# Attention with streaming heads, then a SwiGLU block: masks and sums shared between VectorE and GpSimd, scaling split in two, another written order

## The chip, the cores and the metric

The kernel runs on one core of one Trainium2 chip. A core has TensorE (PE, matrix products), VectorE (DVE), ScalarE (ACT), GpSimd (POOL) and SyncE (SP, which here only starts transfers). Each engine takes its own instructions strictly in order; semaphores make one wait for another. The metric is the device time of one execution, in microseconds (us).

## What is computed

Four batches, eight heads, 768 positions, 64 values a head. Three heads look at all earlier keys, five ("streaming") at four sink keys and a window of 64. The result is laid out as 3072 rows of 512 and goes through a gated feed-forward block of width 1536.

```python
scores = scale * np.matmul(q, k.transpose(0, 1, 3, 2))
stream_keep = causal & (is_sink | in_win)
mask = np.where(retr[0, :, 0, 0, None, None], full_mask, stream_mask)
scores = np.where(mask[None, :, :, :], scores, -1000000000.0)
a = np.exp(scores - np.max(scores, axis=-1, keepdims=True))
a = a / (np.sum(a, axis=-1, keepdims=True) + 1e-09)
attn = np.matmul(a, v)                       # -> x: 3072 x 512
g = x @ w_gate
out = (g * (1.0 / (1.0 + np.exp(-g))) * (x @ w_val)) @ w_out
```

## The kernel before

**Tiles.** The 3072 rows are 24 tiles of 128. Tiles come in pairs (tiles 2n and 2n+1 of pair n), with one load each of q, k and v (v is called x in the load names). Four tiles make a group for the feed-forward block; there are six groups, 0 to 5.

**Attention.** For each pair q and k are cast to f16 (`cq`, `ck`), turned by PE (`trq`, `trk`, L466) and copied out of PSUM (`evq`, `evk`); v is cast (`cx`, four pieces). For each tile there are two to four units of scores. PE makes a unit (`sc`, L560, matmuls that use 64 rows), ACT takes the exponential (`ex`, L569), and POOL multiplies units 0 and 1 by a 0/1 mask (`mask`, L577; for the first four tiles PE adds the mask itself). PE then makes the values (`val`, L587, odd heads and even heads), with a column of ones that yields the sum. DVE takes the reciprocal of these sums and scales (`nm`: L594 and L595 in one task), PE turns the result (`xtr`, L606), and it is copied out as the group's input (`xe`). `sk` and `sv` copy the sink keys and values beside each key tile.

**Feed-forward.** For each of a group's 12 blocks j PE makes a gate and a value product (`gate`, `vals`, L732; four matmuls of 512 columns, in group 0 for j under 4 in halves of 256). ACT makes a tanh (L738), DVE two fused multiplications (`stt1` L742, `stt2` L748), which leave h in f16. Groups 0 to 4 use a fast product: seven block products (`p1` to `p7`, L812) in place of eight, for which sums of blocks of h (`hs`, L799, each in two parts of 768 columns) and of the output weights (`ws`, L412, 512 columns) are needed. DVE adds the products up (`oe`, L828), and SP or ACT stores them. Group 5 uses the plain product (L766), so that the end is short.

**Weights.** Six loads each of the gate, value and output weights (`load g`, `v`, `o`), cast to f16 by one of three engines (`wc`).

**Order.** Nothing is scheduled at run time or by the compiler. Every task is added with a list of engines that may do it, what it depends on, and the buffers it takes. Three strings then say everything: `ORDER` is the order in which all tasks are issued (two characters a task), `WAYS` picks the engine from the task's list (0 is its first), `SLOTS` the buffer of each ring. Numbers over 3700 in `ORDER` are warm-ups: matmuls on the identity whose result nobody uses. Since every engine is in order, `ORDER` also sets what waits behind what on it.

**Buffers.** PSUM is eight banks (`gv`, `o` take one, `big` takes two). A bank is free for the next gate when its `stt` has run.

Of the kernel before, what the change touches and what calls it, by code (L numbers as in the profile page):

```python
# [13 lines left out]


ORDER = (
    "0706090A0C001W1X02041U1V03xx1f1gy21c1h2021yG28292A1d1e011i1j051p1q1r1w1s22232B2C2DzG2E2F2N2O2L2M"
    "2S2W2c2d081b1Z1a1Y1t1u1v1k1l1m0D2X2f2g2o2h2p2i0B2624252G2H272I2P2Q0G3D2j2k2l2t2m2n0F1n2R1y2J2K1z"
    "1o2U2V0m11103C3I3J3K2e2x2y30311x9G9L0g0y9D9E9F980z9I9J9H9K9M999A0h9B9C3L3M3N139X9Y9Z9S9T9U9c9d9e"
    "32383R3S3O9N9O0n149V9W9P9a9b9k9f9g0E2Y2Z2b2a2q3P2r2s2u0o179p9h9i9j9l0i169m9n9o9q3b33343U3V9r9s9t"  # L20
    "9Q9R2z353637390k1C3i3j0l1FALAMAN3Q9u9v3T0j3W3X3f3gAGAHAI3l3n0H3E3F3Y3Z3m3o3a3GABACA6A72v3A0q1DA9"
    "199w3h0r1G3H3k0K3x3y3wA8AA9x9yAOAPAJAKA10I3uAE0J3v3c3pA20p2w0w1E3dADAFATAV3B1A0s123q3r3z4344450x"
    "1HA3409zA03s3tA44142494A4647484B3eB4BEB7B5B6BdBFBGBeB8BgA5ASAU0v1B1KAx0u181Q4H4O4C4DBfBh0M4bAuAv"
    "Aw0S0t151M1OAyBJBKBL4L4M4WBTBUBV0L4aBM2TBC0Y7E4P4QApAqBWBXB9BABBBDArBN1SBYBZBaAQAXARAW4j4k4lBbBc"
    "Bi1IBjBk1R1T4g4h4i0V4E4F4GBHBI1N1P1J1L0O5IAsAt0P5J0R4R4S4N4m4n4o0Q5N5K5M4s4t0W6X0N4c4d4eAeAYAa4p"
    "4z4q4rAZAzB0B1B2B35p5R5S5T53AcAdAi0eAfAj0UAgAhAkAo4I4T54554U4V4XBOBPBQ0ZBlBm56574u4v5O5P5QBRBS5v"
    "5w5x584w4x4y50BnBo595A5B5C5f5gBv5q4J4K51524f5D5E7I5FAbAlAm5G5H4Y5c5l5dBp0T5u5s6Y5U5VBqBsC50c5h0f"
    "4ZCMCNCOD5D6ClCoD7CmCnCp5yBrC1AnBw5t5z60617F627M7N7OD0D1D264656CBtBxD8D9CbCcCdBuByBzC0666G6H6ZC2"
    "C66J6R5L6WD3D4C3C4C7CBCgChCi5e5i6K5j5m5kCvCwCPCQCx6e6f6gCjCk5W5X5Y5Z7HCCCDCECyCz6M6N67686V6b6c6d"
    "7m6aCeCf6L630X8TCFCG5r696A6B6DC8C95a5n5o5b6E6F6I6O6P6S6QCHCICJCqCrCs8R7D7J7K7L6T6UCA6h6i6jCtCu7n"  # L30
    "CWCXCYCKCLDCDE0a7kEDEEEFCRCSCTEGEHENEOEP6p6qCZCa6n6o6k6u6l6mCUCVDDDFDeDfDg7176777P7Q7REIEJEKELEM"
    "DhDi6r6s6t6v7273EQERESET0b7l7q7r7sDADGDBDHEU7a7b7c7X7Y7Z7g7t7u7v6w6xDyDzE0E1E2DZDaDbDtDuDvDcDd74"
    "756yDwDxDMDN7G7S7T7d7e7f6z707UDoDpDqDIDJDKDL7z80817o82837wDjDkDlDrDsE8E9EA8Z8a8b78797x7y7A7i7jE3"
    "7p8SE67BEBEC7V7WDODPEVEW7h848586E4E5E70d8Q7CF9FLFMFN8U878E8F8G8H8IDQDRFOFP8W8X8B8C8DDSDUDYDTFEDV"
    "DWDX8YDmDn8M8c8k8l8d8eFfFgFhFaFbFcEaFBFCFDFFFdFe8f8p8gFpFqFrF6F7F8FAEfEXEYEgFQ888J8K8L8i8j8NEZEb"
    "FGFHFI8V8hEdEhFn8w8x8y9192FkFlFiFjFmFoFsFtFRFS8m8n8oEwExFVFWFXFJFK8qFTFU8z908t8uEcElEeEiEsEjEkEm"
    "F1F2F3EnEo898r8A8s8O8v9394Ep959697EzF48PGsEyF0GgGqErEvFxEqH0GtGuGxGyFzEtEuGbF5GzH1GdGeGfGhGnGoGp"
    "GrGRGYGZGaGOGPH2H3GcGQGSH4H7H8FYFZH9FwFyGvGwGlFuG0FvGiGjGkGWGmGAGTGUGVGXH5H6HFGJGKGLG1G6G7HAG2G3"
    "G4G5GMGNG8G9GBHBGCHCHDHEHGGFGDGGGHGEGIHHHIHJHMHNHKHLHOHRHSHTHWHUHXHPHQHVHYHZHbHaHcHd"
)  # L40
WAYS = (
    "000011000000000000000000000000000000000000000000000000000000221222212202000222120000000000001212"
    "222200000000000000000000000010222212011011000000000000002200222202010000000000000000001000000000"
    "001000022220011000000000000000002000000000000000000202000000000000000000002000000000000000001111"
    "020000000000000000000020000000000000000111002100001000000001000000000020100200001000000000000000"
    "020000000000000220022110000000000000000000000101000000000000001200020001011000000000000000001200"
    "010221000011000000000001201000000000001001201020000010000000000000020000000000000000000000000000"
    "000000000000000000000000000000000000000000000000000000000000000000000000000000000000000000000000"
    "000000000000000000000000000000000000000000000000000000000000100000000000000000000000000000000000"
    "000000000000000000000000000000000000000000000000000000000000000000000000000000000000000000000000"  # L50
    "000000000000000000000000000000000000001000000000000000000000100000000000000000000000000000000000"
    "000000000000000000000000000100000000000000000000011000000000000000000000000000000000000000000000"
    "00000000000000000000000110000000000001"
)
SLOTS = (
    "010523746398924140017A691538054937A26015867A243A0728A5610106041104122604230063425254461240012220"
    "616021634560623213222642160414454362206033410246145620040626321320124465214360460626441622432440"
    "621165236020212616240613644563623432261644260400045616443601212225622426021013212562406111646123"
    "602404160624445624226160436133025200041115011401001041120010140250100510251151104002111142021000"
    "105010103111210300242114110200231013211051242020002001131000011010421000101111021203013411510201"  # L60
    "101101230243003552112201121013112000112013502441205021100020210100201431500242103300140100104010"
    "0112151133105202030222114230520231200001302031053100312120042120200121014011300412010"
)
# [56 lines left out]
def kernel(  # L120
# [89 lines left out]
    def recast(task, dst, src):  # L210
# [370 lines left out]
    def values(t, odd):  # L581
        if t not in avs:
            avs[t] = buf("big", [128, 2, 512], FP, "av")
        for n in range(4):
            bl = av_blocks.pop((t, 2 * n + odd))
            for m, (ee, vv) in enumerate(bl):
                nc.tensor.matmul(avs[t][:, odd, n * 66:n * 66 + 65], ee, vv,  # L587
                                 start=(m == 0), stop=(m == len(bl) - 1))

    def norm(t):  # L590
        xb = xbs[t] = buf("xb", [128, 4, 2, 64], FH, "xb")
        rc = small.tile([128, 2, 4, 1], FP, name="rc", tag="rc")
# [1 line left out]
        nc.vector.reciprocal(out=rc, in_=av[:, :, :, 64:65])  # L594
        nc.vector.tensor_tensor(  # L595
            out=xb.rearrange("p n o d -> p o n d"), in0=av[:, :, :, 0:64],
            in1=rc.to_broadcast([128, 2, 4, 64]), op=ALU.mult)
# [395 lines left out]
```

## Time and profile before

| what | us |
|---|---|
| median of three runs (255.04 to 255.12) | 255.06 |
| the profiled execution's own time | 255.12 |
| its span, first to last instruction | 253.3 |
| PE busy | 245.6 |
| POOL busy | 187.1 |
| DVE busy | 179.9 |
| ACT busy | 159.0 |

The span is shorter than the time by what lies before the first instruction and after the last. Busy time of PE includes the flight of a matmul through the array, so successive matmuls of 512 columns show as 379 ns each while they start every 216 ns. The page cuts the span into 40 slices of 6.3 us; a digit is the busy share in tenths. In the groups, a line is: source line, engine, operation, out<-in by the program's names, shapes, count, then busy us and the mean ns of one, then the idle time before it and what ended that. In the chain, a line is start, length, engine, tile and line.

### The profile page before, as it was taken

Reading aid. Unit: us, or ns where it says so; the run is one execution under the profiler, and the core shown is the slowest. Engines: PE = TensorE matmul, PEld = TensorE weight load, DVE = VectorE, ACT = ScalarE, POOL = GpSimd, SP = SyncE. Lnnn points to the kernel's source line nnn. Section 1 sums busy time; section 2 is a strip of 40 time slices with the busy share of each in tenths; the row PEclk is TensorE's granted clock in tenths of the full one; section 3 lists DMA queues with packets and bytes.
Section 4 is the critical chain, followed back from the end, with each engine's and each line's share of the span. In section 5 each row is a group of like instructions: output and inputs, shape, how many; then the busy total and the mean of one; then the engine's idle time right before and its main releaser. Section 6 shows DMA issues by size and latency. Waiting matters only on the chain.

```text
span 253.3 us, 5948 instructions
## 1 busy us (share of the span) xinstructions
PE 245.6 (97%) x2367; PEld 153.3 (61%) x2367; DVE 179.9 (71%) x319; ACT 159.0 (63%) x256; POOL 187.1 (74%) x168
## 2 busy tenths in 40 slices
PE   7988999999999999999999999999999999999995
PEld 2666855554566786665654657666465774466743
DVE  1469789759899964888676767785686576875740
ACT  5797879988767689867996675644746222511002
POOL 6689999899999999999638997856699532073400
PEclk9999999999999999999999999999999999999999
DMA  7999999999930294005270000002200004000053
GB/s 193 359 353 338 346 330 354 385 387 355 311 121 0 72 280 150 5 0 168 71 262 0 3 0 3 0 3 82 86 4 0 3 0 155 14 0 3 0 194 137
DMA packets 32331, 34.98 MB, mean 138 GB/s; under 512 B 1456, under 2 KB 22192, under 8 KB 32304
## 3 DMA queue, kind: packets, MB, share of 16 engines
q1 hardware_dynamic: 31200, 32.71, 40.3%
q10 hardware_dynamic: 1104, 1.90, 2.0%
q8 instruction: 18, 0.29, 0.5%
q14 instruction: 9, 0.07, 0.1%
HBM read 28.31 MB, written 6.29 MB: 137 GB/s over the span
## 4 chain that ended last, share of the span: by engine, by line
PE 58%; POOL 26%; SPq 4%; issue 3%; DMA 3%; ACT 2%; DVE 2%; POOLq 0%; DVEq 0%; ACTq 0%
PE banks L732 33%; PE banks L812 11%; POOL e L577 9%; POOL h_sb L799 7%; POOL wt_sb L412 5%; PE banks L766 4%; PE banks L560 4%; PE banks L587 4%; SPq L349 3%; DMA raw<-in_k_dram 3%; POOL hs_sb L799 2%; PE banks L466 1%; POOL vt L208 1%; PE banks L606 1%; DVE sil L742 1%
## 5 line engine op out<-in xcount | busy, mean ns | idle before, releaser
L577 POOL TENSOR_TENSOR e<-e,m 128x1024 f16<-128x1024 f16 (+1 forms) x38 | 67.3, 1783 | 19.2 <-ACT e L569 19.2
L738 ACT ACTIVATE sig<-banks 128x512 f32<-128x512 f32 (+1 forms) x76 | 43.2, 577 | 50.3 <-PE banks L732 39.0
L732 PE MATMUL banks<-xt,wv_sb 128*128 128x512 f16 (+1 forms) x304 | 72.0, 368 | 0.3 <-POOL wv_sb L208 0.2
L569 ACT ACTIVATE e<-banks 128x1024 f16<-128x1024 f32 (+2 forms) x68 | 59.5, 910 | 20.0 <-PE banks L560 10.9
L732 PE MATMUL banks<-xt,wg_sb 128*128 128x512 f16 (+1 forms) x304 | 71.5, 368 | 0.1
L742 DVE SCALAR_TENSOR_TENSOR sil<-sig,banks 128x512 f32<-128x512 f32 (+1 forms) x76 | 49.4, 657 | 26.1 <-ACT sig L738 23.9
L748 DVE SCALAR_TENSOR_TENSOR h_sb<-sil,banks 128x512 f16<-128x512 f32 (+1 forms) x76 | 49.1, 655 | 7.7 <-PE banks L732 5.3
L732 PEld LDWEIGHTS <-wv_sb 128*128 128x128 f16 x304 | 28.5, 98 | 28.3 <-issue 0.5
L732 PEld LDWEIGHTS <-wg_sb 128*128 128x128 f16 x304 | 27.8, 98 | 27.6 <-issue 0.9
L812 PEld LDWEIGHTS <-h_sb 128*128 128x128 f16 x360 | 34.5, 98 | 7.8 <-POOL wt_sb L412 0.6
L799 POOL TENSOR_TENSOR h_sb<-h_sb 128x768 f16<-128x768 f16 x20 | 32.7, 1641 | 5.2 <-PE banks L812 4.1
L828 DVE TENSOR_TENSOR out_sb<-banks,out_sb 128x512 f32<-128x512 f32 x35 | 23.9, 689 | 10.3 <-PE banks L812 9.7
L799 POOL TENSOR_TENSOR hs_sb<-h_sb 128x768 f16<-128x768 f16 x10 | 16.3, 1643 | 18.9 <-DVE h_sb L748 13.4
L812 PE MATMUL banks<-wt_sb,h_sb 128*128 128x256 f16 x180 | 22.1, 273 | 0.4 <-DVE out_sb L828 0.4
L812 PE MATMUL banks<-wo_sb,h_sb 128*128 128x256 f16 x180 | 21.9, 273 | 0.0
L560 PE MATMUL banks<-qT,kT 64*128 64x128 f16 x472 | 21.5, 218 | 0.5 <-DVE xb L595 0.5
L560 PEld LDWEIGHTS <-kT 64*128 64x128 f16 x472 | 14.4, 94 | 11.9 <-issue 10.6
L587 PE MATMUL banks<-vt,e 128*128 128x65 f16 x472 | 18.2, 193 | 0.9 <-DVE rc L594 0.4
L587 PEld LDWEIGHTS <-e 128*128 128x128 f16 x472 | 16.8, 97 | 3.6 <-issue 0.7
L595 DVE TENSOR_TENSOR xb<-banks,rc 128x512 f16<-128x512 f32 x24 | 16.6, 691 | 0.9
L799 POOL TENSOR_TENSOR h_sb<-hs_sb,h_sb 128x768 f16<-128x768 f16 x10 | 16.3, 1642 | 0.2
L466 PE MATMUL banks<-ident,hq 128*128 128x128 f16 x192 | 14.6, 219 | 0.6 <-ACT hq L206 0.6
(55 smaller groups left out, 239.7 us busy)
## 6 DMA issues: line engine op xcount, KB each, us to landing
raw<-in_v_dram SPq DMA_DIRECT2D x12, 512.0 KB, 7.2
raw<-in_q_dram SPq DMA_DIRECT2D x22, 256.0 KB, 5.0
raw<-in_k_dram SPq DMA_DIRECT2D x22, 256.0 KB, 6.0
out_dram<-out_sb SPq DMA_DIRECT2D x7, 512.0 KB, 3.2
raw<-in_moe_w_val_dram SPq DMA_DIRECT2D x6, 512.0 KB, 8.5
raw<-in_moe_w_gate_dram SPq DMA_DIRECT2D x6, 512.0 KB, 8.2
raw<-in_moe_w_out_dram SPq DMA_DIRECT2D x6, 512.0 KB, 8.3
out_dram<-out_sb ACTq DMA_DIRECT2D x3, 512.0 KB, 2.9
```

The lines of the kernel that those rows point to most:

```text
L466: nc.tensor.transpose(tr[:, j], hqs[n, kd][:, j // 4, j % 4], ident)
L560: nc.tensor.matmul(sc[:, c:c + n, :], weights, moving, start=first, stop=last)
L569: nc.scalar.activation(out=to, in_=src, func=AF.Exp, scale=scale)
L577: ENG[task().way].tensor_tensor(out=ev, in0=ev, in1=mm, op=ALU.mult)
L587: nc.tensor.matmul(avs[t][:, odd, n * 66:n * 66 + 65], ee, vv, start=(m == 0), stop=(m == len(bl) - 1))
L732: nc.tensor.matmul(ps, wsb[:, kk, j * 128:(j + 1) * 128], xt[:, kk, c[0]:c[1]], start=(kk == 0), stop=(kk == 3))
L738: nc.scalar.activation(out=sg[g, j, c], in_=gs[g, j, c], func=AF.Tanh, scale=0.5)
L742: nc.vector.scalar_tensor_tensor(out=sl[g, j, c], in0=sg.pop((g, j, c)), scalar=1.0, op0=ALU.add, in1=gs.pop((g, j, c)), op1=ALU.mult)
L748: nc.vector.scalar_tensor_tensor(out=hs[g, j][:, c[0]:c[1]], in0=sl.pop((g, j, c)), scalar=0.5, op0=ALU.mult, in1=vs.pop((g, j, c)), op1=A ...
L799: ENG[T_hs[g, x][part].way].tensor_tensor(out=to, in0=a, in1=b, op=op)
L812: nc.tensor.matmul(rooms[g, p][:, x], left[:, j, 128 * x:128 * x + 128], right[:, j], start=(j == 0), stop=(j == NK - 1))
L828: nc.vector.tensor_tensor(out=cell(*to), in0=rooms[g, p], in1=cell(*other), op=ALU.add)
```

## The change

All three strings are replaced. Masks, sums of blocks of h and sums of weights may go to DVE or POOL (before: POOL alone). Of 38 masks 15 go to DVE, of 40 sums of h 19, of 12 sums of weights 4. The reciprocal becomes a task of its own (`rc`), and the scaling (`nm`) may go to DVE or ACT; on ACT it is eight instructions, one for each head. Tiles 13 and 23 are scaled by ACT. Some casts, evacuations and sink copies change engines too, the loads come in another order, and there are 27 warm-ups, not 23. The mask's and the sums' code is the same; it takes the engine from the task.

```diff
-            T_ws[x].append(P.add(f"ws{x}.{i}", ["POOL"],
+            T_ws[x].append(P.add(f"ws{x}.{i}", ["DVE", "POOL"],
...
+    def inverse(t):
+        rc = rcs[t] = small.tile([128, 2, 4, 1], FP, name="rc", tag="rc")
+        av = avs[t][:, :, 0:264].rearrange("p o (n x) -> p o n x", x=66)
+        nc.vector.reciprocal(out=rc, in_=av[:, :, :, 64:65])
+
     def norm(t):
         xb = xbs[t] = buf("xb", [128, 4, 2, 64], FH, "xb")
-        rc = small.tile([128, 2, 4, 1], FP, name="rc", tag="rc")
+        rc = rcs.pop(t)
         av = avs.pop(t)[:, :, 0:264].rearrange("p o (n x) -> p o n x", x=66)
-        nc.vector.reciprocal(out=rc, in_=av[:, :, :, 64:65])
+        if T_nm[t].way == "ACT":
+            for o in range(2):
+                for n in range(4):
+                    nc.scalar.activation(out=xb[:, n, o], in_=av[:, o, n, 0:64],
+                                         func=AF.Copy, scale=rc[:, o, n])
+            return
         nc.vector.tensor_tensor(
             out=xb.rearrange("p n o d -> p o n d"), in0=av[:, :, :, 0:64],
             in1=rc.to_broadcast([128, 2, 4, 64]), op=ALU.mult)
...
-                ms.append(P.add(f"mask{t}.{u}", ["POOL"],
+                ms.append(P.add(f"mask{t}.{u}", ["DVE", "POOL"],
...
-        nm = T_nm[t] = P.add(f"nm{t}", ["DVE"], (lambda t=t: norm(t)), deps=vals, takes=["xb"])
+        rcp = P.add(f"rc{t}", ["DVE"], (lambda t=t: inverse(t)), deps=vals)
+        nm = T_nm[t] = P.add(f"nm{t}", ["DVE", "ACT"], (lambda t=t: norm(t)), deps=[rcp],
+                             takes=["xb"])
...
-                    f"hs{g}.{x}.{part}", ["POOL"],
+                    f"hs{g}.{x}.{part}", ["DVE", "POOL"],
```

The first loads in the two orders, before and after:

```
k0 q0 q1 k1 q2 x0 k2 x1 k3 q3 v0 g0 g1 v1 x2 v2 g2 g4 g5 g3 x3
k0 q0 q1 k1 q2 x0 x1 k2 q3 g1 g0 v0 v1 x2 k3 g2 v2 g5 k4 g4 x3
```

More of the change, by code (lines that the diff above doesn't have):

```diff
@@ L16 @@
 ORDER = (
[L17 to L36, printed above, removed]
@@ L37 @@
-    "F1F2F3EnEo898r8A8s8O8v9394Ep959697EzF48PGsEyF0GgGqErEvFxEqH0GtGuGxGyFzEtEuGbF5GzH1GdGeGfGhGnGoGp"
-    "GrGRGYGZGaGOGPH2H3GcGQGSH4H7H8FYFZH9FwFyGvGwGlFuG0FvGiGjGkGWGmGAGTGUGVGXH5H6HFGJGKGLG1G6G7HAG2G3"
-    "G4G5GMGNG8G9GBHBGCHCHDHEHGGFGDGGGHGEGIHHHIHJHMHNHKHLHOHRHSHTHWHUHXHPHQHVHYHZHbHaHcHd"
+    "0302071W1Xxx1f061U000104051Vy61c1g1h092223yD2A2B2C1dzG1i1j0A2425yD2D1e1s1t1q1r1y2E2F2G2H2O2P0C2a"
+    "2g2h2i081Z1b1Y1k1l1m1n1a1u1v1w1x1z2Q2W2R1o1p20210B2629272I2J2K2L0D2b2j2k2lyU2m2s2t2n2p2y2q2M2N28"
@@ new lines @@
+    "2S2T2U2V0F3I3O3P3Q0h13A0A1A20g0m0n0E0G380y9W9X9Y0i0o390l0J0k32339q9r109Z9a2Y2ZA5A69b9v2r2o112f2d"
+    "A79w9s9c2c353E360H14A3A49t9u9dA8A99y9x9z2e0z9g3J3R3S3T349h9i16379l9m9n0r172u2v2z2w2x9o9p3a3bAAAB"
+    "AC3A3B3C3D3F1F3X3Y3U3i3V3ZADAE9e9f3W3c3d3u3vAjAkAl1C3KAFAGAH3p3qAIAJAZAa3M9j9k1G3L3e3f3j3g3h3s3t"
+    "3r3m3n3oAeAUAVAWAmAnAh30313k3l0q0jAfAgAi0u18Ab3N3w3x3y3z19AKALAPAQAR434B4C4D1DAcAdAM0p1AANAO0I42"
+    "4840413G3HArAtASATAXAYAq494E4A4F4G4H4I4J0x4QBcBdBeBfBg0P5VBIBJBK0t150M4lBNBOBP2X4U4V4WBwBxByC1C2"
@@ new lines @@
+    "BX0v0w1E1MBY0K46454447BzC0BZBaBbC30d4K4L1H1S1Q1R1T4X4g4YBLBM0s12C6C7C8C4C54Z0W6n6o4t4u1N1PBSBTBU"
+    "4M4N4O4PBVBWBQBR0U1BAw1K1I0L4k4q4r4sBhBiBj4vAoApAx1J1L0ZC9CA4a4b4z50AsAu0O5UAvAzBmBnBo1O5d5eBG0R"
+    "63514w5A4x4yBDBEBFBH5fBrBsBtB0B10N4o4p4n0cB2B34m54555EB4B54R4c4d4e5F5G4f4hB6B7B8CECG5H5I52535MBu"
+    "Bv5a5b5cBkBl0T675J5657585B595N696A6BAyCB0V6m0a5K5L0S645s5t5p5q5zBpBqCD66B9BA0Y7W5O5P7Z865Q7Y6CBC"
+    "CC4S4i4j5C5R4T840Q5W5Y5X5Z5D6D6ECJCFCPCHCLBBCK5S5TCTCICM6F6I6J6R6KDODPDQ0fCaCbCcCpCqCrDTDU6GDRDS"
@@ new lines @@
+    "DV7e7f7g5uD9DA685r5v5w5x5yCdCeDBCNCOCQDCDD5g5h5i6b6cDWDXCRCSCV0X7V6HCkClCm5j5k5l5m6Y6Z6aD4D5D6DE"
+    "DFCsCt0b856L6MCUDG606V6W6h6X658rCnCfCgCoCh6u6v8A8B8CDHDI6w6N6O6S6P6QCzD0D1DJDK6p5n5o61626T6UCiCj"
+    "DL6d6e6i6f6g6l6rCWCXCY6s6t6x6y707B716z726j6kCuCvElEmD2D3En7b7c7dD7D8DaCwDcDMDNEbEcEd73747tCZEoEp"
+    "7u7vCxCyDbDdEHEIEJ757h7i8D8E8FEeEfEgEhEi767XEKEL8qDYDZDf7N7q80De777r7s78797A7C7OEMENEO7aDgDhDi7I"
+    "7J7K8G8H7FDxDyDzE27w7G7x817y7zE0E1E5EjEk7j7H8J8S8K8L7LE3E4E6Dm7k7l7M7m7nE7E8E9DkDl7D7E7o7p8283Eq"
@@ new lines @@
+    "ErEs8m0e6q7P7Q7RERESEPDj7S7T7U8nEWEXEQETEUEVEY8s8t8uEtEuFZFaFb8Z8a8b8W8XDnEFECED8IEZEaEEEG8c8d8M"
+    "8NFjFkFlFmFn8p8v8w8x89EAEBFcFd878O8P8Q8R8o8YFUFVFWDoDp8i8y8z9697919C92938TG3G4G5DqDrEyF0ExEzDsDw"
+    "88G6FtFuFvDtDuG7FeFfFgG8G9FXFYGA90FhFiDvGBGCGDGEGFFoFpFq8e8f8g8h8j9495F3FrFs9G9H9I9O9PEvEwF4F1F2"
+    "FyFzG09M9J98999K9L9A9B9NG1G2F5F6FKFLFMFNFOF7F8F9FAFBFCFPFQFRFS9D9Q9R9S8U8k8l9E9FGGGHFG9T9U9VFDFE"
+    "FHFFFJ8VHBH6H7H8HOHaGpHbHEHCFIGLGNFTHDGwGxH9HFGyHLHMHQHAHNHPHGHHHIHVHWGzH0HXHRGIGPGJHYHZHSHJHKHc"
@@ L40 @@
+    "GrGsHdHeGtFwFxGKGMH1H2H3GmGnH4HTHUGoGkGQGRGTGhGiGaGWH5GjGlGuGvGqGOGSGUGdGVGYGXGbGZGcGgGeGfHfHgHh"
+    "HiHjHkHlHmHnHpHqHoHrHsHuHvHwHzHtHxHyI0I1"
 )
 WAYS = (
[L42 to L50, printed above, removed]
@@ L51 @@
-    "000000000000000000000000000000000000001000000000000000000000100000000000000000000000000000000000"
-    "000000000000000000000000000100000000000000000000011000000000000000000000000000000000000000000000"
-    "00000000000000000000000110000000000001"
+    "000010000000000000000000000000000000000000000000000000000000222112220202202202100100111101111101"
+    "212201100000000000000000001000212222200000110000000000000000200012102000000000000100000002000010"
+    "010000002201222212011011000001000000001100000001000000000122221000000000000100000002010010000000"
@@ new lines @@
+    "002200020002001000001001000000002001001001000000000020021200001100000000000100100012201011001000"
+    "010001000000000120000100000000002002200220000000010010000000001000000000000000001000000010001001"
+    "000000001001000011000202200000100010000000001101001000000000220000102200000100100000000000210000"
+    "000000000001000000000000000000000000000000000000000000000000000000000000000000000000000000000000"
+    "010100001000000000000000000000000000000000000000000000000000000000000000000000000000000111100000"
@@ L54 @@
+    "000000000000000000000000000000000000000000000000000000000000000000000000010101000001000000000001"
+    "000000000000000000000000000000000000000000000000000000000000000111011000000000000000100000000000"
+    "000000000000000000000000000000000000000000000000000010111000110000000000001000000000000000000000"
+    "00000000000000000000000000000000000000000000000110000000000000"
 )
 SLOTS = (
-    "010523746398924140017A691538054937A26015867A243A0728A5610106041104122604230063425254461240012220"
@@ L57 @@
[L57 to L61, printed above, removed]
@@ L62 @@
-    "0112151133105202030222114230520231200001302031053100312120042120200121014011300412010"
+    "010523647283946A70A07A201493928725670A9428701531018A92510106060106241210230223620444560040024221"
+    "606131646543222121141604224604206541636104312624461602060436561321406142656462420434221601300142"
+    "622125646134200614064604424563620010241606465210021642360615403443622414260332304562246201206163"
+    "602130565244042213614560436242111100130212110301321100000012410101002301411234000011010220115315"
@@ L63 @@
+    "010430222023310241132011111050140100412110130111202215133220110001501114000112101021024501031041"
+    "012102011210114001000411005020511021030111001121110011202500035103215102501142011111010042025401"
+    "1011051040011102431112024051512010041113012011142000312001150125512411125114202130120"
 )
```

## The prediction, made before the changed kernel was run

> **What bounds the kernel now.** I read the page's first two parts, then busy time by stretch, then the chain of waits, then the groups by shape.
>
> ```profile
> PE 245.6 (97%) x2367; PEld 153.3 (61%) x2367; DVE 179.9 (71%) x319; ACT 159.0 (63%) x256; POOL 187.1 (74%) x168
> PE   7988999999999999999999999999999999999995
> DVE  1469789759899964888676767785686576875740
> POOL 6689999899999999999638997856699532073400
> DMA  7999999999930294005270000002200004000053
> ```
>
> TensorE (PE) works in 245.6 of 253.3 us. Only its first four slices and its last are below 9. The other engines have 25 to 37% free over the whole span. The DMA row is full for the first 70 us: there the inputs arrive.
>
> ```profile
> core 0: us, PE busy (x) PEld busy (x) DVE busy (x) ACT busy (x) POOL busy (x), PEclk, DMA share, GB/s
> 30.00:80.00 50.00, 49.78 (x477) 28.90 (x474) 42.54 (x77) 42.40 (x67) 48.47 (x41) 1.00 0.90 296
> 80.00:130.00 50.00, 49.15 (x560) 33.75 (x559) 37.86 (x70) 39.74 (x65) 43.62 (x30) 1.00 0.39 114
> 130.00:180.00 50.00, 50.00 (x488) 30.32 (x487) 35.27 (x62) 30.82 (x48) 37.78 (x32) 1.00 0.10 36
> 180.00:230.00 50.00, 49.90 (x394) 29.60 (x392) 37.08 (x61) 19.63 (x33) 29.21 (x18) 1.00 0.06 22
> ```
>
> From 30 to 230 us PE is idle for 0.22 + 0.85 + 0 + 0.10 = 1.17 us. GpSimd (POOL) is nearly full from 30 to 80 (48.47 of 50), VectorE (DVE) has 7.46 us free there.
>
> ```profile
> 52.26 0.86 PE banks L732 x4
> 55.51 3.48 POOL e L577 x2
> 63.40 3.38 POOL wt_sb L412 x3
> 134.26 0.21 PE banks L560 x3
> 134.47 0.97 PE banks L732 x4
> ```
>
> The chain runs through POOL between 55 and 113 us, for 26% of the span. The first lesson is that this share isn't a gain waiting to be had: PE was just as full there, so two engines were tied, and relief for one leaves the other. The last two lines show a second cost: four matmuls take 0.97 us right after the 64-row score matmuls of L560 and 0.86 otherwise. By the starts of successive matmuls each switch between 64 and 128 rows costs about 0.095 us.
>
> **The change part by part.** Real PE work is the same: every matmul but the warm-ups is there in the same number. Warm-ups rise from 23 to 27, 4 x 0.216 = 0.86 us; they stand before the first inputs (k0 lands at 5.0, q0 at 6.8, q1 at 8.1 us, in the same load order up to x0), and I cost them at nothing. Uncovered they would cost that 0.86.
>
> *Switches.* Read in the written order, PE changes between 64 and 128 rows 78 times, not 82: 4 x 0.095 = -0.4 us.
>
> *The start.* After x0 the loads go x1, k2, q3, g1, g0, v0, v1, x2, k3 in place of k2, x1, k3, q3, v0, g0, g1, v1, x2. A load of x takes 1.77 us of the DMA stream, one of q or k 1.36, a weight 1.5. From x0's landing at 12.65 that puts q3 at 17.1 and g1 at 18.6, or 1.4 later each, if the gap of 2.1 us that stands before k3's first half now (usual: 0.7) stays. POOL casts g1 (1.04), so the first gate starts at 19.7 to 21.1 instead of 23.49. But POOL's queue then holds, one behind the other, halves of g0 and v0 (0.62 each), mask4.1 (1.40), v1 (1.04), a block of x2 (0.61), g0's other half (0.62), k3 (1.04, landing 26.3 to 27.7), mask5.0 (2.13), mask5.1 (1.40): that ends at 30.8 to 32.3, val5 waits for it, then the cast of v2 at 31.8 to 33.3 and vals0.4 for that. Adding PE's tasks behind these (0.86 for a gate, 0.44 for a half, 0.3 to 0.55 for scores) the 25th us of real PE work is reached at 34.4 to 35.9 us. In the kernel before that mark is vals0.1.256, at 35.53. So -1.1 to +0.4; I take -0.5.
>
> *Masks and sums.* 38 instructions move from POOL to DVE: 7 masks of 1024 elements, 8 of 640, 19 sums of 768, 4 of 512.
>
> ```profile
> L577 POOL TENSOR_TENSOR e<-e,m 128x1024 f16<-128x1024 f16 x20 | 42.5, 2128 | 15.1 <-ACT e L569 15.1
> L577 POOL TENSOR_TENSOR e<-e,m 128x640 f16<-128x640 f16 x18 | 25.2, 1400 | 4.1 <-ACT e L569 4.0
> L799 POOL TENSOR_TENSOR h_sb<-h_sb 128x768 f16<-128x768 f16 x20 | 32.7, 1641 | 5.2 <-PE banks L812 4.1
> L412 POOL TENSOR_TENSOR wt_sb<-wo_sb 128x512 f16<-128x512 f16 x6 | 6.8, 1154 | 0.0
> L208 DVE COPY xt<-banks 128x512 f16<-128x512 f16 x16 | 6.2, 416 | 2.3 <-PE banks L606 2.3
> L748 DVE SCALAR_TENSOR_TENSOR h_sb<-sil,banks 128x512 f16<-128x512 f32 x68 | 45.9, 683 | 7.3 <-PE banks L732 5.3
> L594 DVE RECIPROCAL rc<-banks 128x8 f32<-128x8 f32 x24 | 4.8, 202 | 1.7 <-PE banks L587 1.3
> L595 DVE TENSOR_TENSOR xb<-banks,rc 128x512 f16<-128x512 f32 x24 | 16.6, 691 | 0.9
> ```
>
> POOL loses 7 x 2.128 + 8 x 1.400 + 19 x 1.642 + 4 x 1.155 = 61.9 us. That can buy no more than PE's 1.2 us of idle time in the middle. On DVE no row has two f16 inputs from SBUF. Nearest from below: the f16 copy, 512 elements in 0.416. With a fixed 0.151 (from stt rows of 256 and 512 elements, 0.418 and 0.685) that makes 0.681, 0.483, 0.549 and 0.416 for the four sizes, 20.7 us in all. From above: the f32 rate of 0.685 for 512, so 1.219, 0.819, 0.952 and 0.685, 35.9 in all. Other tasks leave DVE for ACT and POOL (three casts of 1.21, five sink copies of keys and three of values, two scalings, two evacuations, less two added): about -8. DVE goes from 179.9 to 193 or 208, still under PE's 246, and the cost is one of place. Two bounds:
> - The densest place is the middle of group 1. Between nm8 and stt1 of 1.8 DVE has 9.1 us of its usual work and seven of the moved instructions (three of 512, four of 768, of which four in a row), 3.4 to 5.9; together 12.6 to 15.0. PE's tasks in the same stretch are six gates and values of 0.86, two of the same at its head (1.7), two products of 1.31, two transposes of 0.45 and three units of scores: 11.8. DVE falls behind by 0.8 to 3.2 us, and behind it stt1 of 1.7, 1.0 and 1.8 wait, each holding a bank that a later gate needs. A lead of DVE's could cover it: 0 to 3.2. I take 1.3.
> - The other 31 take 17 to 30 us where DVE has a quarter of its time free. Below: all hidden, and the 1.2 us of idle PE goes too (-1.2). Above: a third of what the 15 masks take at the slow price (15.1) shows, 5.0, since a val stands right behind each. I take 0.8, near the lower end, for PE waits little on anything in the rows of 130 to 230.
>
> The Trainium skill, "SBUF — State Buffer", section "Who interferes with whom", has a rule against this part: a VectorE instruction with two SBUF inputs and a GpSimd instruction that reads SBUF exclude each other, and the later one waits until the other has ended. No row here shows it, for every two-input DVE instruction of this kernel takes one of them from the banks. By that rule, with POOL busy half the time in pieces of about 1.7 us, an estimate is 38 x 0.5 x 0.85 = 16 us more on DVE, and the time would be some 259.
>
> *The split of the scaling.* For 22 tiles reciprocal (0.202) and scaling (0.691) remain on DVE, mostly side by side: nothing. For tiles 13 and 23 ScalarE (ACT) makes eight scalings of 128x64; nearest ACT rows are 0.19 to 0.20 (copies of 4 and 8 elements) and 0.27 (128x128), so 1.6 to 2.1 us for 0.69. Behind nm23 waits xtr23; PE has three transposes (0.67), vals4.11 (0.86) and out3.p3 (1.31) = 2.8 to do first, as against 0.2 + 2.1. Nothing, and at most 1.4 if that cover is gone. ACT has 40% free there.
>
> *The end.* Twelve times four matmuls of 0.216 and a last small store, as now: nothing.
>
> **Sum.** On the profiled execution's own 255.12 (span 253.3 and 1.8 around it; the median is 255.06): -0.4 - 0.5 + 1.3 + 0.8 = +1.2, so 256.3.
>
> **Rivals.** A measurement of this kernel can tell 0.2%, 0.5 us, from no change.
> 1. Forecast, 256.3 (own range 255.6 to 258.5): the added DVE work holds up gates somewhere between 40 and 110 us. Chance 0.45.
> 2. DVE becomes the bound up to the end of group 1: the slow price holds, and masks' and sums' lateness adds up. -0.9 + 3.2 + 2 to 5 gives 259.4 to 262.4; I say 259.5. For: DVE at 42.5 of 50 from 30 to 80 now. Against: the casts taken off it (three of 1.21) stand in that very stretch. 0.15.
> 3. Faster: the weights' earlier landing is kept. Its place is the first gate, its price -1.1 at the 25-us mark, with -0.4 for switches and -0.4 for idle PE in 80 to 130 where POOL was late: 253.2. It decides if that mark comes before 34.9 us and PE then loses under 1.5 us more than before. For: 7.5 us of free DVE time from 30 to 80. Against: POOL's queue of casts and masks up to 32 us. 0.26.
> 4. Hidden anyway: PE is the bound on both sides and the terms cancel, 255.0. 0.14.
>
> Faster 0.26, same 0.14, slower 0.45 + 0.15 = 0.60. The range of 253.2 to 260.0 leaves out the far ends of 2 and 3.
>
> **What would show it.** First gate at 19.7 to 21.1; the mark of 25 us at 34.4 to 35.9; the moved rows on DVE between 0.416 and 1.22 us; PE idle from 30 to 230 up from 1.2 to over 3 us, waiting for stt or masks; POOL near 130 us busy and of no effect. I'm wrong if that idle time stays near 1.2, or if DVE rows come out above 1.22.

## The result, and the profile after

| what | before | after |
|---|---|---|
| median, us (four runs each) | 255.09 | 256.01 |
| lowest to highest, us | 255.04 to 255.30 | 255.79 to 256.66 |
| the profiled execution's own time, us | 255.12 | 256.02 |
| its span, us | 253.3 | 254.0 |

The ratio is 1.0039, with a 95% interval of 1.0020 to 1.0058: the kernel is slower by some 0.9 us. The forecast was 256.3 with a range of 253.2 to 260.0.

First the page's busy times and slices of the kernel after, in the form shown for the kernel before:

```profile
PE 246.7 (97%) x2371; PEld 154.0 (61%) x2371; DVE 196.5 (77%) x339; ACT 163.9 (65%) x278; POOL 136.0 (54%) x140
PE   7998999999999999999999999999999999999995
DVE  1688989979999978699869878779695957786630
POOL 7387977879867498740643779131654202008300
DMA  6999999999975057200043000000040004000044
```

POOL lost 51.1 us of work, DVE gained 16.6, and PE is as full as it was. Now busy time by stretch (columns as before):

```profile
30.00:80.00 50.00, 49.65 (x481) 28.68 (x479) 45.96 (x78) 41.65 (x67) 39.61 (x38) 1.00 1.00 320
80.00:130.00 50.00, 49.35 (x574) 34.46 (x572) 43.55 (x76) 42.54 (x76) 28.34 (x22) 1.00 0.23 72
130.00:180.00 50.00, 49.78 (x482) 29.67 (x480) 38.65 (x69) 34.25 (x53) 24.69 (x24) 1.00 0.10 33
180.00:230.00 50.00, 49.98 (x389) 29.74 (x387) 38.45 (x62) 19.78 (x38) 15.77 (x11) 1.00 0.12 43
```

PE's idle time from 30 to 230 us is 0.35 + 0.65 + 0.22 + 0.02 = 1.24, against 1.17 before. DVE is now the one that is nearly full early, 45.96 of 50. The shares of the chain that ended last, before and after, tell the same:

```profile
PE 58%; POOL 26%; SPq 4%; issue 3%; DMA 3%; ACT 2%; DVE 2%; POOLq 0%; DVEq 0%; ACTq 0%
PE 76%; DVE 12%; ACT 8%; issue 3%; POOL 0%; DVEq 0%; ACTq 0%; POOLq 0%
```

POOL was relieved of a quarter of its work and left the chain, DVE and ACT came in, and nothing was won. The moved instructions, by shape:

```profile
L578 DVE TENSOR_TENSOR e<-e,m 128x640 f16<-128x640 f16 x8 | 5.8, 726 | 4.0 <-ACT e L570 3.9
L578 DVE TENSOR_TENSOR e<-e,m 128x1024 f16<-128x1024 f16 x7 | 5.5, 788 | 1.3 <-ACT e L570 1.2
L812 DVE TENSOR_TENSOR h_sb<-h_sb 128x768 f16<-128x768 f16 x9 | 8.0, 900 | 0.3 <-POOL hs_sb L812 0.2
L812 DVE TENSOR_TENSOR h_sb<-hs_sb,h_sb 128x768 f16<-128x768 f16 x5 | 3.7, 767 | 0.0
L812 DVE TENSOR_TENSOR hs_sb<-h_sb 128x768 f16<-128x768 f16 x5 | 3.0, 598 | 0.1
L413 DVE TENSOR_TENSOR wt_sb<-wo_sb 128x512 f16<-128x512 f16 x3 | 2.0, 710 | 0.0
```

A mean hides much here. One by one, a mask of 640 takes 0.48 to 1.09, one of 1024 0.68 to 1.07, a sum of h 0.54 to 1.98, a sum of weights (a fourth is in a row of its own, 793 ns) 0.42 to 1.29. The shorter value is the bare duration; the rest is, as e5 below shows, a wait inside the instruction. Over the 38 the time above the bare durations is about 8.4 us; 16 of them hold nearly all of it.

**Where the 0.9 us is.** Busy time is a poor measure, since a matmul of 512 columns shows 379 ns and starts every 216. The trace gives a better one. Every matmul other than the warm-ups is there in both kernels. Give each the usual distance to the next start for its shape (0.216 us for 512 columns, 0.109 for 256, and 0.040 for the score matmuls that use 64 rows), add these up in order of time, and compare the moments at which the two kernels have done equally much.

| PE work done, us | moment before | after | late by |
|---|---|---|---|
| 1 | 9.21 | 9.36 | 0.15 |
| 13 | 25.63 | 26.10 | 0.48 |
| 40 | 53.83 | 54.19 | 0.36 |
| 60 | 74.08 | 75.04 | 0.96 |
| 80 | 95.24 | 95.99 | 0.75 |
| 90 | 105.75 | 106.99 | 1.24 |
| 120 | 137.01 | 137.51 | 0.50 |
| last matmul | 250.26 | 250.97 | 0.71 |

Half of it is there when 40 us of work are done; the other half is the net of waits that come and go later. The two orders differ, so a mark isn't the same matmul in both: with another distance for the 64-row matmuls the marks at 13, 60 and 90 move by 0.3 us and more, while 0.36 at 40 and 0.71 at the end stay. The remaining 0.2 us of the two times lies outside the spans (256.02 - 254.0 against 255.12 - 253.3).

### The profile page after: what moved, and what is told of

Its sections match the earlier page's. It is cut to its first block, busy times and chain, and to the rows that moved or that the text cites. A ratio compares the mean times of both kernels' runs of the same rounds, so it can differ in the third digit from the quotient of the medians.

```text
span 254.0 us, 5969 instructions
## 1 busy us (share of the span) xinstructions
PE 246.7 (97%) x2371; PEld 154.0 (61%) x2371; DVE 196.5 (77%) x339; ACT 163.9 (65%) x278; POOL 136.0 (54%) x140
## 4 chain that ended last, share of the span: by engine, by line
PE 76%; DVE 12%; ACT 8%; issue 3%; POOL 0%; DVEq 0%; ACTq 0%; POOLq 0%
PE banks L745 41%; PE banks L825 14%; PE banks L561 5%; PE banks L588 4%; PE banks L779 4%; DVE h_sb L761 3%; ACT e L570 3%; PE banks L322 3%; DVE sil L755 3%; PE banks L467 3%; PE banks L617 1%; ACT vt L207 1%; DVE h_sb L812 1%; DVE wt_sb L413 1%; DVE kT L209 1%
## 5 line engine op out<-in xcount | busy, mean ns | idle before, releaser
L578 POOL TENSOR_TENSOR e<-e,m 128x1024 f16<-128x1024 f16 (+1 forms) x23 | 42.2, 1840 | 38.3 <-ACT e L570 38.0
L812 POOL TENSOR_TENSOR h_sb<-h_sb 128x768 f16<-128x768 f16 x11 | 18.4, 1671 | 16.8 <-DVE hs_sb L812 15.5
L812 POOL TENSOR_TENSOR hs_sb<-h_sb 128x768 f16<-128x768 f16 x5 | 8.5, 1709 | 18.7 <-DVE h_sb L761 14.1
L606 DVE TENSOR_TENSOR xb<-banks,rc 128x512 f16<-128x512 f32 x22 | 15.2, 691 | 0.7
L578 DVE TENSOR_TENSOR e<-e,m 128x640 f16<-128x640 f16 (+1 forms) x15 | 11.3, 755 | 5.3 <-ACT e L570 5.2
```

The costliest lines, as they stand in the source:

```text
L578: ENG[task().way].tensor_tensor(out=ev, in0=ev, in1=mm, op=ALU.mult)
L812: ENG[T_hs[g, x][part].way].tensor_tensor(out=to, in0=a, in1=b, op=op)
```

## Experiments

Every kernel below is the one before or the one after with a small edit. Engines are changed, or tasks moved in the written order, by these lines in `order()`:

```diff
+        for t in self.tasks:
+            t.way = next((w for w, names in OTHER.items() if t.name in names), t.way)
...
+        place = {t.name: i for i, t in enumerate(self.tasks)}
+        for name, ahead in MOVES:
+            numbers.remove(place[name])
+            numbers.insert(numbers.index(place[ahead]), place[name])
```

The column "before" is the kernel before as it ran beside that experiment. The kernel after ran 0.92 us above it (256.01 against 255.09), and an edit of it is judged by how its own difference compares with that 0.92.

| run | edit | median, us | before, us | ratio, 95% interval |
|---|---|---|---|---|
| e1_all_pool | after; the 38 back on POOL | 274.72 | 255.36 | 1.0760 (1.0746 to 1.0775) |
| e2_scale_dve | after; tiles 13, 23 scaled by DVE | 257.72 | 255.36 | 1.0094 (1.0078 to 1.0109) |
| e3_before_dve | before; the same 38 on DVE | 281.62 | 255.36 | 1.1041 (1.1022 to 1.1060) |
| e4_before_mix | before; two sums to DVE, a cast to POOL | 256.24 | 255.36 | 1.0043 (1.0031 to 1.0056) |
| e6_after_moves | after; two waits mended in the order | 257.94 | 255.20 | 1.0109 (1.0096 to 1.0123) |
| e8_after_pool2 | after; two sums back on POOL | 256.86 | 255.20 | 1.0070 (1.0056 to 1.0084) |
| e9_before_cast | before; a cast to ACT | 255.10 | 255.20 | 0.9997 (0.9988 to 1.0006) |
| e10_after_xtr | after; the first mend of e6 alone | 255.97 | 255.19 | 1.0040 (1.0024 to 1.0055) |
| e11_after_warm6 | after; 23 warm-ups | 256.00 | 255.19 | 1.0028 (1.0017 to 1.0039) |
| e12_after_cast_warm6 | the same, half of q0 cast by POOL | 256.52 | 255.19 | 1.0048 (1.0036 to 1.0060) |
| e13_after_mask_behind | e10, and one mask put behind | 255.69 | 255.19 | 1.0029 (1.0016 to 1.0041) |

**The disputed price by itself (e5_ports).** A probe in place of the kernel; it leaves out the whole computation and stores zeros. It runs DVE products of two f16 inputs from SBUF (768 elements) alone and beside several kinds of POOL work.

```diff
+    phase(dve_two, 8, None, 0)
+    phase(None, 0, pool_two, 8)
+    phase(dve_two, 12, pool_two, 8)
+    phase(dve_bank, 12, pool_two, 8)
+    phase(dve_two, 12, pool_cast, 8)
+    phase(dve_two, 12, pool_set, 8)
```

> A probe that computes nothing of the reference (its output is zeros): VectorE and GpSimd repeat one instruction each, in six stretches: VectorE's two-input f16 product of 768 elements alone; GpSimd's alone; both together; VectorE with one input in the banks beside GpSimd's product; VectorE's two-input product beside GpSimd's f32 to f16 cast; the same beside GpSimd's memset. Theory A (the two exclude each other when VectorE takes two inputs from SBUF and GpSimd reads): 0.55 and 1.64 alone, and together each pair takes about their sum, 2.2, VectorE's instructions showing up to 2.1; no effect with an input in the banks (0.685) nor beside the memset. Rival (the long VectorE rows, 0.6 to 1.98 us in the changed kernel, come from something else, such as reading late data): 0.55 and 1.64 in every stretch.

| DVE | POOL at the same time | DVE, us | POOL, us |
|---|---|---|---|
| 8 products | nothing | 4.70 | |
| nothing | 8 products | | 13.61 |
| 12 products | 8 products | 17.60 | 14.97 |
| 12 with one input from a bank | 8 products | 8.61 | 13.62 |
| 12 products | 8 casts of 1024 | 12.82 | 10.20 |
| 12 products | 8 memsets | 7.07 | 8.02 |

The last two columns are from a stretch's first start to its last end. Where POOL ends first, the rest of DVE's twelve run alone, so single instructions tell more:

```profile
25.25 1.83 POOL L52 TENSOR_TENSOR pc<-pa,pb 128x768 f16<-128x768 f16 x1
25.61 1.87 DVE L45 TENSOR_TENSOR dc<-da,db 128x768 f16<-128x768 f16 x1
58.03 1.27 DVE L45 TENSOR_TENSOR dc<-da,db 128x768 f16<-128x768 f16 x1
58.96 1.25 POOL L55 CAST pc<-pf 128x1024 f16<-128x1024 f32 x1
```

A product that takes 0.56 us alone takes 1.87 beside POOL products and 1.27 beside POOL casts, eight times each; the four that are left when POOL has ended take 0.56 again. Beside memsets, or with one input from a bank, nothing is lost (0.56; and 0.69, as in the kernel's rows). POOL pays too: a product takes 1.83 for 1.63, a cast 1.25 for 1.04. The two take turns, one instruction each, a pair every 1.90 us; that is less than the 2.2 expected, so they overlap a little at the ends. So the two exclude each other, and the price depends on what POOL does at that moment. That is the rule that the prediction cited from the Trainium skill, "SBUF — State Buffer", "Who interferes with whom", and the probe agrees with it.

**The whole part undone, and done alone (e1, e3).** In the kernel after, all 38 names go back to POOL; in the kernel before, the same 38 go to DVE, with nothing else changed.

```diff
+OTHER = {'POOL': 'mask4.0 mask6.0 ... hs0.1.0 hs0.3.0 ... ws1.0 ws3.0 ws4.0 ws1.2'.split()}   # e1
+OTHER = {'DVE': 'mask4.0 mask6.0 ... hs0.1.0 hs0.3.0 ... ws1.0 ws3.0 ws4.0 ws1.2'.split()}    # e3
```

> The changed kernel with all 38 masks and sums back on GpSimd, at the same places of the same order. Theory A (the cost is in the order's start and its gates, the moved work is needed where it is): GpSimd gets 62 us of work back, less the 26 it has spent waiting or that VectorE did faster, and is near 190 us busy in an order that left it room for 136; masks become late and the time rises to 257 to 260. Rival B (the moved work is what costs): PE's idle time between 30 and 230 us falls from 1.24 us to under 0.8 and the time is 255.2 to 255.7.

> The kernel before, its own order, with the same 38 masks and sums on VectorE. Theory A (moved work costs VectorE its length of 20.7 us and waits of about 8 us for GpSimd, in an order that left VectorE 42.5 of 50 us full between 30 and 80): 255.6 to 257.5, PE idle between 30 and 230 up from 1.17 us to 2 to 3. Rival B (GpSimd's share of the chain was the limit): PE idle falls below 0.8 and the time to 254.2 to 254.8.

Both missed by far: 274.72 and 281.62 us. In e1 POOL has 191.5 us of work, hardly more than the 187.1 of the kernel before, yet it holds 33% of the chain, and the kernel falls behind the one after by 1.8 us at 27 us of work, 2.9 at 60, 10.4 at 80 and 18.7 at the end. In e3 DVE has 25% of the chain and PE waits up to 4.1 us in one place (at 54.4 us). A part of both losses isn't waiting: after such long waits the granted TensorE clock is 0.50 for a while (e1 from 84.4 to 91.2 and from 121.9 to 125.3, e3 from 58.3 to 61.7), and matmuls of 512 columns start every 0.427 us in place of 0.216. By these starts that costs some 3 us in e1 and 1.5 in e3. In the kernels before and after the clock is 1.00 in all four stretches shown. An order is fitted to its assignment of engines. So the price of "38 instructions moved" can't be had by undoing them in either order, and these two runs tell nothing on the 0.9 us; what they show is that order and assignment are one change.

**One part at a time (e2, e4, e8, e9).** Each edit is put on one line here.

```diff
+OTHER = {'DVE': 'nm13 nm23'.split()}                                # e2, on after
+OTHER = {'DVE': 'hs0.1.0 hs1.4.1'.split(), 'POOL': ['cx5.0.1']}     # e4, on before
+OTHER = {'POOL': 'hs1.4.0 hs3.3.1'.split()}                         # e8, on after
+OTHER = {'ACT': ['cx5.0.1']}                                        # e9, on before
```

> The changed kernel with tiles 13 and 23 scaled by VectorE. Theory A: the two scalings on ScalarE are covered, so 256.0, within 0.2. Rival: eight instructions of 0.33 us in place of one of 0.69 make xtr13 or xtr23 late, and the time falls by up to 0.5, to 255.5.

> The kernel before with two sums on VectorE (hs0.1.0 near 59 us, hs1.4.1 near 107) and one cast of values (cx5.0.1) from VectorE to GpSimd. PE's two waits for GpSimd in the kernel before (0.61 us at 80.2 for a sum of weights, 0.33 at 112.9 for a mask) should go, each sum saving GpSimd 1.64 us for 0.55 to 0.9 of VectorE. Theory A (single places matter, not the total): 254.2 to 254.6. Rival (PE is held by something else at the same moments): 255.0 to 255.2.

> The changed kernel with two of its 38 moved instructions back on GpSimd: hs1.4.0 and hs3.3.1, which took 1.81 and 1.98 us on VectorE at 99.2 and 181.7 us in place of 0.55. Theory A (these waits of VectorE hold what stands behind them, and PE): PE's delays against the kernel before at 99 to 102 (0.4 to 0.5) and 181 to 184 (0.2) go, 255.3 to 255.6. Rival (GpSimd's queue is then late for the sink copy behind it, which PE's scores need): 256.0 to 256.6.

> The kernel before with one cast of values (cx5.0.1) on ScalarE instead of VectorE, where it stood with three others ahead of the first addition of group 0's products, for whose bank PE waits at 80.2 us (0.61). Theory A: that wait goes and nothing else moves, 254.4 to 254.7, faster than both kernels. Rival: ScalarE's cast of 0.62 makes an exponential or a tanh late, 255.0 to 255.7.

e2 came out on the wrong side of both expectations, 1.4 us slower than the kernel after by the medians and 1.85 by the marks of its trace. Tile 13's scaling on DVE (0.69 us at 110.45) stands ahead of an `stt2`, and PE waits 0.64 at 111.04; tile 23's costs PE 0.24 at 209.62. A larger wait of 1.21 stands at 181.5, far from both tiles; e8 and e12 have the same one, so it isn't the scaling's own price. So ScalarE's two scalings are worth some 0.9 us where they stand: they are the one part of the change whose worth in its own order a trace shows.

e4 and e9 aim at the kernel before's longest wait of the middle, 0.61 us at 80.19, where an `oe` stands behind four casts of v on DVE. In both that wait goes (-0.5). In e4, outside both its expectations at 256.24, more than that has been lost before: `hs0.1.0` on DVE takes 0.94 at 58.50, because POOL's mask runs until 59.0, and the key copy behind it and what follows hold up PE by 0.64 and 0.36; another 0.77 is lost at 98.34. In e9 nothing is hit at once, but a wait of 0.37 stands at 97.8 (0.27 at 100.25 before), and at 113.16 PE waits 0.74 for a mask on POOL where it waited 0.33: 255.10 against 255.20, no gain. (The run that was traced took 255.69, for it begins 0.64 late at its first inputs; from there on the marks give -0.50, +0.12 and +0.38, which is nothing.) e8 fell in favour of neither theory as I had put them. Without its sum of 1.81 us at 99.23 DVE has room there, yet PE's waits of 0.19, 0.27 and 0.30 between 99 and 102 us stay as they were. In both traces each ends when ACT has ended a copy out of PSUM (in the kernel after at 99.59, 100.08 and 102.01), so DVE's long sum didn't make them. The time is 0.7 to 0.85 higher (by the medians and by the marks), by a wait of 1.21 at 180.7 us, the place that e2 hit as well. The next runs explain it.

**Mending the waits of the kernel after (e6, e10).** The trace of after has two waits that a move in the order should end: 0.79 us at 24.93 (gate products wait for the copy `xe3`, which comes late on DVE) and 0.42 at 68.74 (products wait for ACT's cast of o3).

```diff
+MOVES = [('xtr3', 'vals0.0.0'), ('xe3', 'vals0.0.0'), ('wc o3', 'cx8.0.0')]   # e6
+MOVES = [('xtr3', 'vals0.0.0'), ('xe3', 'vals0.0.0')]                          # e10
```

> The changed kernel with two places of its order mended: xtr3 and xe3 ahead of vals0.0 (PE waits 0.79 us at 24.9 us for xe3), and the cast of o3 on ScalarE ahead of two casts of values (PE waits 0.42 us at 68.7 for it). Theory A (a full PE never makes up a delay, so a delay taken away anywhere comes off the end): -0.35 at the first, -0.42 at the second, 255.2 to 255.4. Rival (the start is bound by the landing of weights, and only the second counts): 255.6.

> The changed kernel with one of the two moves of the run that had both: tile 3's transpose and its evacuation stand ahead of the first value product of group 0; nothing else. Theory A (PE is full, a wait that is taken away at 25 us stays away, unless the shift changes who gets the port later): the wait of 0.79 us at 24.9 falls to about 0.4, and 255.5 to 255.7 follows against 256.0 of the changed kernel (before: 255.1). Rival (any shift of 0.3 us upsets the fitted meeting of VectorE and GpSimd further on, as it did when the cast of o3 was moved too): 256.5 to 258.

In e6 both waits shrink, by 0.41 and 0.25 us, and the kernel is 1.8 us slower than after. At 79.00 POOL starts a mask of 2.12 us, at 79.04 DVE a sum, which now takes 2.49 instead of 0.56; in the kernel after DVE's sum had begun at 79.12 and POOL's mask only at 79.33. PE waits 1.76 behind it. e10 has the first move alone: its gain of 0.41 is there at 26 us and gone by 28, and the time is that of the kernel after, outside both expectations. This is what took it, in the timeline of e10 (start, length, engine, line; its lines are 7 further on, so L585 is the mask, L220 a cast, L762 `stt1`, L752 gate and value products):

```profile
25.09 1.05 POOL L216 CAST wv_sb<-raw 128x1024 f16<-128x1024 f32 x1
25.31 1.37 DVE L585 TENSOR_TENSOR e<-e,m 128x1024 f16<-128x1024 f16 x1
26.60 0.67 DVE L220 TENSOR_REDUCE wv_sb<-raw 128x512 f16<-128x512 f32 x1
27.20 0.73 DVE L762 SCALAR_TENSOR_TENSOR sil<-sig,banks 128x256 f32<-128x256 f32 x2
27.66 0.60 PE L752 MATMUL banks<-xt,wv_sb 128*128 128x256 f16 x4 [0.84 <-DVE sil L762]
```

DVE's mask of tile 4, one of the 38, meets POOL's cast of v1 and takes 1.37 us for 0.68. The cast and the `stt1` behind it are late, and the value product waits 0.84 for the bank. However early DVE comes, it waits for POOL here.

**The start's other suspects (e11, e12).** 23 warm-ups in place of 27 (a 6 for the 10 in the order's string), and then q0's second half cast by POOL, as the kernel before has it, not by DVE after the first half.

```diff
-    "0302071W1Xxx1f061U000104051Vy61c1g1h092223yD2A2B2C1dzG1i1j0A2425yD2D1e1s1t1q1r1y2E2F2G2H2O2P0C2a"
+    "0302071W1Xxx1f061U000104051Vy21c1g1h092223yD2A2B2C1dzG1i1j0A2425yD2D1e1s1t1q1r1y2E2F2G2H2O2P0C2a"
+OTHER = {'POOL': 'cq0.1'.split()}   # e12 alone
```

> The changed kernel with 6 warm-up products in place of the 10 that stand ahead of q0's transposes, so 23 in all, as before. Theory A (what holds q0's transposes is the two casts of q0 on VectorE one behind the other, which end at 8.50 us, not the warm-ups, which end at 8.59): the transposes start at 8.5 instead of 8.59, and 255.9 to 256.0 follows. Rival (the four warm-ups are the cost, 0.86 us): the transposes start at 7.7 to 7.8 and 255.1 to 255.3 follows.

> The changed kernel with 6 warm-ups as in the run before this one, and q0's second half cast by GpSimd beside VectorE, as the kernel before has it. Theory A (the start's lateness comes from the two casts on one engine): the transposes of q0 start at 7.7 to 7.9 us in place of 8.59, part of it is taken back by the landings that follow, and 255.3 to 255.7 follows against 256.0. Rival (the start is set by the later landings and by ScalarE's and VectorE's evacuations up to the first gate): the first gate stays within 0.2 us of the changed kernel's 22.14 and the time at 255.9 to 256.1. If the shift upsets the later meeting of VectorE and GpSimd: 256.5 or more.

e11 is 256.00: the four more warm-ups cost nothing. In e12 the first gate starts at 21.77 instead of 22.14, but e10 has 21.78 with neither edit, so that isn't theirs; and again all of it is gone by 28 us. The cast isn't the start's cost, theory A of e12 falls. e12 is slower by another 0.5, and that is the clearest reading of the case. The kernel after at 179.7 us:

```profile
179.71 0.49 DVE L578 TENSOR_TENSOR e<-e,m 128x640 f16<-128x640 f16 x1 [1.92 <-ACT e L570]
179.72 3.58 POOL L812 TENSOR_TENSOR hs_sb<-h_sb 128x768 f16<-128x768 f16 x2 [4.61 <-issue]
180.20 0.69 DVE L755 SCALAR_TENSOR_TENSOR sil<-sig,banks 128x512 f32<-128x512 f32 x1
```

and e12 at the same place:

```profile
179.42 3.49 POOL L819 TENSOR_TENSOR hs_sb<-h_sb 128x768 f16<-128x768 f16 x2 [4.34 <-issue]
179.68 1.72 DVE L585 TENSOR_TENSOR e<-e,m 128x640 f16<-128x640 f16 x1 [2.27 <-ACT e L577]
181.32 0.68 DVE L762 SCALAR_TENSOR_TENSOR sil<-sig,banks 128x512 f32<-128x512 f32 x1
```

In the kernel after DVE's mask begins 0.01 us ahead of POOL's sum and takes 0.49. In e12 POOL's sum is 0.26 ahead, and the mask takes 1.72, until the first of POOL's two sums has ended; `stt1` comes 1.1 late, and PE waits 1.2. The same 1.72-us mask stands in e8 (from 179.80, POOL from 179.53) and in e2 (from 180.56, POOL from 180.29). What turned it is a gain: none of the three has the wait of 0.38 us that PE has in the kernel after at 176.81, so POOL's sum comes earlier (by 0.30 in e12), while the mask, which follows ACT, hardly moves (0.03). So three unlike edits lost 0.76 us each in this place, by the marks around it; those of e2 and e12 are nowhere near, and of e8's two sums one stands just behind it.

**The mask put behind (e13).** e10's order, and tile 4's mask behind the cast and the two `stt1` that it stood ahead of; it stays on DVE.

```diff
+MOVES = [('xtr3', 'vals0.0.0'), ('xe3', 'vals0.0.0'), ('mask4.0', 'cx2.0.0')]
```

> The run with tile 3's transpose moved, and besides tile 4's first mask (1024 elements, one of the 38 moved to VectorE) put behind the two gate products and the cast of v0's second half that it stood ahead of; the mask stays on VectorE. In the runs before this one whatever the start gained (0.4 to 0.8 us by 26 us) was given back where group 0's second value products start, at 27.5 to 27.66 us whatever came before. Theory A (what fixes that time is this mask: VectorE waits in it until GpSimd's cast of v1 has ended, 1.37 us for 0.68, and the cast and the gate product behind it come late): those value products start at 26.8 to 27.1 us, and 255.2 to 255.6 follows if the gain is kept. Rival 1 (the time is fixed by the landing of the weights or of k3, not by the mask): they start within 0.15 us of 27.6, and 255.9 to 256.0. Rival 2 (the gain is there at 30 us and goes again at the next meeting of VectorE and GpSimd): earlier by 0.4 or more at 30 us, the time 256 or more, and the trace shows where.

```profile
25.00 1.04 POOL L216 CAST wv_sb<-raw 128x1024 f16<-128x1024 f32 x1
25.54 0.68 DVE L220 TENSOR_REDUCE wv_sb<-raw 128x512 f16<-128x512 f32 x1
26.34 0.75 DVE L762 SCALAR_TENSOR_TENSOR sil<-sig,banks 128x256 f32<-128x256 f32 x2
26.98 1.27 PE L752 MATMUL banks<-xt,wv_sb 128*128 128x256 f16 x10
27.02 0.68 DVE L585 TENSOR_TENSOR e<-e,m 128x1024 f16<-128x1024 f16 x1
```

In e13's timeline the cast and `stt1` go beside POOL's cast without loss, the value products start at 26.98 instead of 27.66, and the mask, now between two POOL casts, has its bare 0.68. At 28 us of time e13 is 0.53 ahead of the kernel after (0.12 of it from the first inputs on, which land a little earlier or later in every run); a wait of 0.37 at 28.19 takes most of that back, a later one of 0.25 (at 35.68 in after) is gone, and from there on e13 is 0.31 to 0.33 ahead at every mark up to the end. Its median is 255.69, 0.3 below that of the kernel after and still 0.5 above the kernel before. The times alone don't show this gain: two of its twelve runs took 256.46 and 257.41, and its ratio of 1.0029 is that of e11, which moves nothing. It rests on the marks of the one trace (255.70). Theory A holds for the place; its 255.2 to 255.6 was too much by 0.1. No version here beats the kernel before.

## Why the prediction came out as it did

The direction was right, and the time within 0.3 us. The cause named first, added DVE work that holds up gates between 40 and 110 us, is right at most for a part. Half of the lateness (0.36 of 0.71) has arisen before, in the start, where a gain was forecast; and of PE's waits between 40 and 110 us those that DVE ends come to 0.87 us against 0.61 before, those that ACT ends to 1.18 against 0.27. How the 0.9 us divides is read from the traces; no run here takes a part away and reaches the kernel before.

- **Switches, -0.4.** Right: 78 of them at 96 and 92 ns (medians for the two directions), four fewer, -0.38.
- **Warm-ups at nothing.** Right, shown by e11.
- **The start, -0.5.** Wrong, and with the wrong sign: +0.36 at 40 us of work. The first gate came at 22.14 us, not at 19.7 to 21.1, and the prediction's mark at 25 us of work (35.53 before; its count runs ahead of the table's) at about 36.0, past the 34.4 to 35.9 given. The 23.49 that it compares the first gate with is the kernel before's first value product; its first gate starts at 24.37. The failed step is "so the first gate starts at 19.7 to 21.1". POOL's cast of g1 did end at 21.03, but PE's own queue was not there yet: it had waited 0.56 at 17.17 for DVE and 0.73 at 18.93 for ACT's key copy, which stood behind an exponential and a cast. After the gate I followed POOL's queue to 32 us and left out DVE's, where `xe3` (0.79) and tile 4's mask were. That this mask holds a part of the start is shown by e13 against e10, which differ by it alone: 0.25 us by the marks. What the rest of the +0.36 is made of is not settled.
- **Bare prices of the 38.** The lower bounds were right to 0.02 us: 0.68, 0.49, 0.55 and 0.42 in the instructions that meet no POOL work. DVE's total of 196.5 is in the range of 193 to 208, POOL's 136.0 is near 130.
- **The exclusion.** I gave it as a rule with an estimate of 16 us and kept it out of the sum. It is real (e5, and the 0.49 against 1.72), but costs about 8.4 us of DVE time, half the estimate, for many of the 38 meet POOL idle. Most of the 8.4 is hidden; what shows is what stands ahead of an `stt` that PE needs.
- **Group 1's dense place, +1.3, and the other 31, +0.8.** Mis-sized. PE's waits of over 0.13 us after 36 us sum to 2.74, against 1.77 before: +0.97 for both. The dense place shows 0.65 (0.29 at 81.98 and 0.36 at 82.50, on a DVE queue that had four sums in a row), but the kernel before had lost 0.61 at the same place to its casts, so the net there is nothing. The other 31 show little on DVE: 0.22 at 104.78, behind a mask of 0.96, and later 0.38 at 176.81 and 0.19 at 183.96. The sum has no term for waits on ACT; four waits that ACT ends, 1.18 in all (0.42 for its cast of o3 and the three between 99 and 102), are the largest part in the kernel after, and e8 shows the three to be there without DVE's sum. The terms as measured give -0.38 + 0.36 + 0.97 = 0.95, where the matmuls end 0.71 late: 0.24 isn't accounted for.
- **Scaling on ACT at nothing.** Right: eight in 1.75 us, in the 1.6 to 2.1 given, and e2 shows that DVE could not have done them as cheaply in this order.
- **What would show it.** "PE idle from 30 to 230 up from 1.2 to over 3" was wrong (1.24). The prediction had said "I'm wrong if that idle time stays near 1.2", so by its own sign it failed, and single DVE instructions went above the 1.22 of its other sign too (up to 1.98; the means of the rows are 0.60 to 0.90). The first sign was badly chosen: PE's idle time rose by 0.07 us where the waits between starts rose by 0.97, since the flight of the matmuls covers them, and 0.9 us was never going to show as 2.

So the closeness is in part luck, two errors that cancel: 0.9 too good at the start, 1.1 too much in the middle. The faster rival failed on its own condition, the mark before 34.9 us. DVE as the bound failed too: at 196.5 us it had room, and lost only by position. "Hidden anyway", 255.0, missed by 1.0 us.

## What to carry to other kernels

When one engine is full, a wait that it meets stays to the end as a step unless a later wait shrinks for it, and relief of another engine (51 us of POOL, 26% of the chain before) buys nothing by itself. Compare two kernels by the moment at which the full engine has done equal work: the steps show each wait, and whether a mend is kept. In a hand-written order, engine and place are one choice; where two engines exclude each other, put the instruction that can wait behind those that the full engine needs, as e13 did, and expect any shift upstream to decide such meetings anew.

## What the runs showed of the hardware

- A POOL cast (one input) excludes a DVE product of two SBUF inputs too, and is itself slowed: 1.27 us for 0.56 on DVE, 1.25 for 1.04 on POOL (e5). A POOL memset is not affected (0.95 each) and does no harm.
- Who starts first has it, and the later one waits for a whole instruction of the other: 0.49 or 1.72 us for the same mask. In the kernel after the lead is 0.01 us by the profile, whose times on POOL are rough. Two of e10's six runs (256.82 and 256.92 us) and two of e13's twelve (256.46 and 257.41) lie as far above the others as one or two such lost meetings cost; they were not profiled, so that this is their cause isn't shown.
- The granted TensorE clock was 0.50 for 3.4 to 6.8 us at and after PE's waits of 2.9 to 4.1 us in e1 and e3; there a matmul of 512 columns started every 0.427 us.
